# A convolution with an expert layer behind it: where the experts' weights are split into a high and a low part

## The chip, the cores and the metric

The kernel runs on one core of a Trainium2 chip. The core has five engines with a queue of instructions each: TensorE (PE, matrix products), VectorE (DVE), ScalarE (ACT), GpSimd (POOL) and SyncE (SP, which here only issues transfers). An engine takes its instructions strictly in the order in which they were put into its queue; a transfer is issued by an instruction in such a queue, too, and is then carried out by 16 DMA engines that all queues share. The metric is the device time of one execution in microseconds (us); less is better.

## The reference

A long convolution along the sequence, by Fourier transforms, and behind it a layer of eight experts of which each token takes one:

```python
Xf = np.fft.rfft(x, n=L, axis=1); Hf = np.fft.rfft(h, n=L, axis=0)
y = np.fft.irfft(Xf * Hf[None, :, :], n=L, axis=1)[:, :S, :]     # 8 x 5696 x 128
...
logits = y @ w_gate + modality_bias[modality_id]                 # 45568 tokens, 8 experts
e_idx = np.argmax(logits, axis=1)
...
for e in range(E):
    h = np.maximum(y[mask] @ w1[e], 0.0)                         # 128 -> 1024
    out[mask] = gate_w[mask, None] * (h @ w2[e])                 # 1024 -> 128
```

All is float32. The kernel makes a product of two float32 matrices out of three fast passes: each operand is split into a high part (the value rounded to the fast type, a ScalarE copy) and a low part (the value less its high part, a VectorE subtraction), and high x high, high x low and low x high are added up. For the experts this needs both parts of all weights.

## The kernel before

The batch is done in two groups of four sequences. **Stage 1** and **stage 2/3** (`stage1`, `stage23`) transform a group, multiply with the filter and transform back half way; `stage23` is a loop over 64 frequencies k, in which PE makes `px` (L261) and `pu` (L239), VectorE and GpSimd the products `t` (L264, L271), and ScalarE copies `pu` from the accumulators to `ut` (L244, and `hs`, L224), which is stored. **Stage 4** (`stage4`) finishes tokens, computes their expert and scatters each token as a row into a table sorted by expert. The **expert part** (`Moe`) then takes tiles of 512 tokens of one expert from that table. Its 104 tiles come in four levels, a level being what can be done with the tokens scattered so far: level 0 has 18 tiles, level 1 18, level 2 45, and level 3 23 small ones. Level 0 and 1 run beside the rest of stage 4; level 2 and 3 run alone.

An expert tile takes eight steps f (level 3: four). In a step PE makes three products into `ph` (`gemm1`, L567 to L569), ScalarE takes the high part of its positive values to `hh` (L572), VectorE the low part to `hl` (L573), and two steps later PE uses both in three products into `po` (`gemm2`, L589 to L591). `ph` has two buffers, so `gemm1` of step f+2 waits until `hl` of step f is done. The tile's weights lie in one of three slots (`slot`, 2 MB each with both parts of both matrices), used in turn; jobs are dealt so that a slot mostly keeps its expert, and the load of a slot (L543) is skipped when its expert stays the same.

`presplit` (L445 to L454) writes the split weights into a scratch in main memory, `w12s`, in 16 pieces: load 512 KB into `ws` (L450), ScalarE copy (L451), VectorE subtraction (L452), store 1 MB (L453). The transfers are issued from ScalarE's queue. There is one `ws` buffer, so a load waits until the store before has landed. `presplit` runs beside `stage23` of the second group (L673); the `0.25` there is its share in `run_all`, which deals out steps of several generators in turn.

What `run_all` fixes is the order in which work is written down. A scheduler then puts the instructions of PE, DVE, ACT and POOL into an order of its own, by its own estimate of times; in the expert part SP's queue alone keeps the order in which it was written.

Of the kernel before, what the change touches and what calls it, by code (L numbers as in the profile page):

```python
# [10 lines left out]
F32 = mybir.dt.float32  # L11
F32R = mybir.dt.float32r
# [3 lines left out]
ALU = mybir.AluOpType  # L16
AX = mybir.AxisListType
PACED = mybir.DependencyInfo(mybir.DependencyClass.Sync, mybir.DependencyReason.DATA)
PSUM = bass.MemoryType.PSUM
# [3 lines left out]
E, FF = 8, 1024  # L23
# [12 lines left out]
QA = 27  # L36
HP = 1000
PACE = 2
S4R = 5
RATE = 1.05  # L40
# [14 lines left out]
JOBS = [(lv, j) for lv, n in enumerate(LEVELS) for j in range(n)]  # L55
# [6 lines left out]
NSLOT = 3  # L62
# [19 lines left out]
def conv_moe(  # L82
# [5 lines left out]
    nc = tc.nc  # L88
# [353 lines left out]
            nc.vector.tensor_copy(bases[0], bases[1])  # L442


    def presplit(sp):  # L445
        for e in range(E):
            for a in range(2):
                s = sp.tile([128, 2, FF], F32R, name="ws")
                v = s.bitcast(F32)
                nc.scalar.dma_start(v[:, 1], w12_d[e, :, a])  # L450
                nc.scalar.copy(s[:, 0], v[:, 1])  # L451
                nc.vector.tensor_tensor(s[:, 1], v[:, 1], v[:, 0], op=ALU.subtract)  # L452
                nc.scalar.dma_start(w12s[e, :, a], v)  # L453
                yield  # L454


    padt = cp.tile([128, NSUB, RW], F32, name="padt")
# [62 lines left out]
    class Moe:  # L520
        def __init__(self, wp, sp, pst, psh, pso):
            self.sp, self.pst, self.psh, self.pso = sp, pst, psh, pso
            self.slots = [wp.tile([128, 2, 2, FF], F32R, name=f"slot{i}") for i in range(NSLOT)]
            self.st = {}
            self.outs = []
            self.tabs = {}

        def load(self, t):
# [6 lines left out]
            nc.sync.dma_start(rt[:, :ns], src[bass.ds(r0, ts), :].rearrange("(p c) w -> p c w", c=ns))  # L535
            self.st[t] = {"rt": rt, "ts": ts, "ns": ns}

        def load_weights(self, t):
            lv, j = JOBS[t]
            tab, n = self.tabs[lv][0], LEVELS[lv]  # L540
            ex = nc.sync.value_load(tab[0:1, n + j:n + j + 1], min_val=0, max_val=E - 1)
            ch = nc.sync.value_load(tab[0:1, 2 * n + j:2 * n + j + 1], min_val=0, max_val=1)
            nc.sync.dma_start(self.slots[t % NSLOT].bitcast(F32), w12s[bass.ds(ex, 1)].rearrange("o p a i f -> (o p) a i f"), cond=ch > 0)  # L543

# [74 lines left out]
        def run(self):  # L619
            LAG = 2  # L620
            total = len(JOBS)
            steps = []
            for t, (lv, j) in enumerate(JOBS):
                n = 4 if lv == len(LEVELS) - 1 else 8
                steps += [(t, f, n) for f in range(n)]
            self.load(0)
            self.load_weights(0)
            self.load(1)
            self.load_weights(1)
            self.load(2)  # L630
            self.prep(0)
            for g in range(len(steps) + LAG):
                t, f, n = steps[g] if g < len(steps) else (total, g - len(steps), 4)
                if f == 0 and t + 3 < total:
                    while JOBS[t + 3][0] not in self.tabs:
                        dispatch(4)
                        yield
                    self.load(t + 3)
                if t < total:
                    self.gemm1(t, f)  # L640
                    dispatch(1, self.st[t]["act"])
                    self.scatter(1, self.st[t]["act"])
                else:
                    self.scatter(1)
                if g >= LAG:
                    self.gemm2(*steps[g - LAG][:2])
                if f == LAG - 1 and t + 2 < total:
                    self.load_weights(t + 2)
                if t + 1 < total:
                    if f == (4 if n == 8 else 1):  # L650
                        self.prep(t + 1)
                if f == LAG and t >= 1:
                    self.finish(t - 1)
                yield
            if t < total or f < LAG:
                self.finish(total - 1)
            self.scatter(len(self.outs))
# [5 lines left out]
    with tc.tile_pool(name="p4", bufs=2, space=PSUM) as ps4, \  # L663
            tc.tile_pool(name="p4l", bufs=1, space=PSUM) as ps4l:
        with tc.tile_pool(name="s2", bufs=2) as sp2, tc.tile_pool(name="p2x", bufs=3, space=PSUM) as psx, \
                tc.tile_pool(name="p2u", bufs=2, space=PSUM) as psu:
            with tc.tile_pool(name="s1b", bufs=2) as sp1:
                run_all((stage23(0, sp2, psx, psu), 3), (stage1(1, sp1, ps4, ftab), 2))
            fx.close()
            tp = ctx.enter_context(tc.tile_pool(name="table", bufs=1, side="right"))  # L670
            sp4 = ctx.enter_context(tc.tile_pool(name="s4", bufs=2, side="right"))
            with tc.tile_pool(name="ws", bufs=1) as wsp:
                run_all((stage23(1, sp2, psx, psu), 3), (stage4(0, sp4, ps4, ps4l, 0, QA, True), S4R), (presplit(wsp), 0.25))  # L673
            dispatch(len(queue))

        def fence():

            nc.gpsimd.dma_start(rows_d[E * REGION:E * REGION + TS, :].rearrange("(p c) w -> p c w", c=NSUB), padt)

        ev = [None] * (len(LEVELS) + 1)  # L680
        with tc.tile_pool(name="moew", bufs=1) as wp, tc.tile_pool(name="moe", bufs=2) as sp, \
                tc.tile_pool(name="pm1", bufs=1, space=PSUM) as pst, tc.tile_pool(name="pm3", bufs=2, space=PSUM) as psh, \
                tc.tile_pool(name="pm2", bufs=2, space=PSUM) as pso, tc.manual_schedule(engines={mybir.EngineType.SP}):
            moe = Moe(wp, sp, pst, psh, pso)

            def level(lv, src):
                tab, ev[lv] = table(tp, lv, ev[lv - 1])
                moe.tabs[lv] = (tab, src)

            s4 = stage4(0, sp4, ps4, ps4l, QA, NQ)  # L690
            for _ in range(AHEAD):
                next(s4)
            fence()
            level(0, views[NVIEW])

            def rest():
                yield from s4
                while queue:
                    yield
                fence()  # L700
                level(1, views[NVIEW])
                yield from stage4(1, sp4, ps4, ps4l, 0, NQ)
                while queue:
                    yield
                padrow = tp.tile([1, E], I32, name="padrow")
                nc.vector.tensor_copy(padrow, bases[0][0:1, :])
                for e in range(E):
                    r0 = nc.sync.value_load(padrow[0:1, e:e + 1], min_val=e * REGION, max_val=e * REGION + NTOK)
                    nc.sync.dma_start(rows_d[bass.ds(r0, TS), :].rearrange("(p c) w -> p c w", c=NSUB), padt)
                level(2, rows_d)  # L710
                level(3, rows_d)
            run_all((rest(), RATE), (moe.run(), 1))


def _constants():
# [80 lines left out]
```

## Time and profile before

| what | us |
|---|---|
| median of 3 runs | 2305.79 (2302.34 to 2326.87) |
| profiled execution | 2318.76, its span 2317.0 |
| stage 2/3 of the second group, with `presplit` in it | 391 to 665 |
| the same stage after `presplit` has ended | 665 to 865 |
| level 0 of the experts beside stage 4 | 890 to 1245 |
| level 1 beside stage 4 | 1245 to 1520 |
| level 2, alone (a stretch of it) | 1560 to 2060 |

The stretches are read from the first and last instructions of the lines named above. In the profile an engine is busy while an instruction of its own computes; issuing a transfer, or standing at an instruction that waits, does not count as busy. TensorE runs at one of two clocks, and the granted clock of a stretch is the mean, with 1.00 for full speed. Matmuls overlap in the profile, so a busy time of PE is read as an upper bound, and its waits are the better measure of what it loses.

### The profile page before, as it was taken

How to read it: one execution, taken by the hardware profiler on the slowest of the kernel's cores; microseconds unless marked ns; L12 is line 12 of the kernel's file. 1: busy time of each engine (PE TensorE's matmuls, PEld its weight loads, DVE VectorE, ACT ScalarE, POOL GpSimd, SP SyncE). 2: the span in 40 equal slices, each digit the busy share in tenths (PEclk: the TensorE clock that was granted, in tenths of full speed). 3: DMA queues.
4: the chain of work that ended last, by engine and by line, in shares of the span. 5: the costliest groups of instructions: out<-in, count | busy, mean ns of one | idle time of the engine just before them, and what ended most of it. 6: DMA issues, size and time to landing. Idle time of an engine off the chain costs nothing.

```text
span 2317.0 us, 33168 instructions
## 1 busy us (share of the span) xinstructions
PE 2107.8 (91%) x9598; PEld 1502.3 (65%) x9598; DVE 1466.0 (63%) x2473; ACT 1132.8 (49%) x2010; POOL 1085.6 (47%) x1050
## 2 busy tenths in 40 slices
PE   6779999899999897999899989889999999999997
PEld 5655555334444445777677667667888888888886
DVE  6559999776777984576465555555555555555443
ACT  6557776333333343555455555334444444444433
POOL 2126655344777763665665556553333333333222
PEclk9899999999999997999999999979999999999999
DMA  9999989899997765433244432132111121123331
GB/s 338 325 307 318 312 293 301 290 314 320 300 282 240 230 193 214 130 109 113 88 149 149 150 101 85 55 123 80 44 47 42 45 82 44 45 80 109 106 104 56
DMA packets 198309, 388.89 MB, mean 168 GB/s; under 512 B 32757, under 2 KB 63833, under 8 KB 193776
## 3 DMA queue, kind: packets, MB, share of 16 engines
q1 hardware_dynamic: 148832, 276.81, 36.5%
q10 hardware_dynamic: 25776, 62.34, 8.5%
q0 software_dynamic: 23520, 47.61, 6.2%
q8 instruction: 78, 1.28, 0.2%
q14 instruction: 103, 0.84, 0.1%
HBM read 393.95 MB, written 174.21 MB: 245 GB/s over the span
## 4 chain that ended last, share of the span: by engine, by line
PE 56%; issue 3%; ACT 2%; DVE 2%; another core or an unknown queue 2%; DMA 1%; POOL 1%; SPq 0%; POOLq 0%; ACTq 0%; DVEq 0%
PE ph L567 8%; PE ph L569 7%; PE po L589 7%; PE po L590 7%; PE po L591 7%; PE ph L568 7%; PE py L357 4%; PE pxt L602 2%; PE pxt L550 2%; PE py L364 1%; PE pl L371 1%; DVE hl L573 1%; ACT hh L572 1%; PE pu L239 1%
## 5 line engine op out<-in xcount | busy, mean ns | idle before, releaser
L573 DVE SCALAR_TENSOR_TENSOR hl<-ph,hh 128x512 fp32r<-128x512 f32 x740 | 506.7, 689 | 457.1 <-ACT hh L572 361.7
L572 ACT ACTIVATE hh<-ph 128x512 fp32r<-128x512 f32 x740 | 440.9, 599 | 600.0 <-PE ph L569 410.5
L613 POOL DMA_INDIRECT out<-of,mrt x370 | 363.1, 981 | 576.7 <-ACT hh L572 475.5
L298 POOL DMA_INDIRECT rows<-rt,idx x360 | 375.3, 1042 | 274.5 <-ACT hh L572 163.5
L271 POOL TENSOR_TENSOR t<-t,t 96x512 f32<-96x512 f32 x212 | 296.7, 1416 | 223.9 <-DVE t L264 214.4
L589 PE MATMUL po<-hh,slot 128*128 128x512 f32 (+1 forms) x832 | 328.3, 395 | 42.3 <-ACT hh L572 25.7
L264 DVE TENSOR_TENSOR t<-px,hs 96x512 f32<-96x512 f32 x512 | 318.2, 676 | 61.5 <-PE pu L239 17.4
L567 PE MATMUL ph<-mxh,slot 128*128 128x512 f32 (+1 forms) x832 | 331.1, 398 | 17.7 <-DVE hl L573 8.1
L590 PE MATMUL po<-hl,slot 128*128 128x512 f32 (+1 forms) x832 | 313.4, 377 | 0.1
L569 PE MATMUL ph<-mxh,slot 128*128 128x512 f32 (+1 forms) x832 | 312.1, 375 | 0.8 <-issue 0.8
L568 PE MATMUL ph<-mxl,slot 128*128 128x512 f32 (+1 forms) x832 | 312.7, 376 | 0.0
L591 PE MATMUL po<-hh,slot 128*128 128x512 f32 (+1 forms) x832 | 310.6, 373 | 0.0
L261 PE MATMUL px<-z,m 96*96 96x512 f32 x512 | 261.5, 610 | 11.1 <-DVE t L264 5.8
L589 PEld LDWEIGHTS po<-hh,slot 128*128 128x128 f32 x832 | 159.3, 192 | 82.4 <-ACT hh L572 36.5
L244 ACT COPY ut<-pu 90x512 f32<-90x512 f32 x256 | 145.0, 583 | 132.6 <-PE pu L239 60.3
L239 PE MATMUL pu<-t,mi 96*96 96x512 f32 x352 | 182.9, 625 | 20.7 <-ACT ut L244 11.4
L567 PEld LDWEIGHTS ph<-mxh,slot 128*128 128x128 f32 x832 | 159.7, 192 | 53.9 <-DVE hl L573 18.5
L590 PEld LDWEIGHTS po<-hl,slot 128*128 128x128 f32 x832 | 158.8, 191 | 35.5 <-DVE hl L573 2.7
L569 PEld LDWEIGHTS ph<-mxh,slot 128*128 128x128 f32 x832 | 159.1, 191 | 31.4 <-issue 0.5
L591 PEld LDWEIGHTS po<-hh,slot 128*128 128x128 f32 x832 | 158.7, 191 | 30.0
L568 PEld LDWEIGHTS ph<-mxl,slot 128*128 128x128 f32 x832 | 159.9, 192 | 23.6 <-issue 0.5
L261 PEld LDWEIGHTS px<-z,m 96*96 96x96 f32 x512 | 82.2, 166 | 115.4 <-issue 64.3
(157 smaller groups left out, 2892.2 us busy)
## 6 DMA issues: line engine op xcount, KB each, us to landing
slot<-w12s SPq DMA_DIRECT2D x104, 2048.0 KB
z<-z SPq DMA_DIRECT2D x256, 180.0 KB
z<-z SPq DMA_DIRECT2D x90, 320.0 KB
z<-z SPq DMA_DIRECT2D x90, 256.0 KB
ua<-ut SPq DMA_DIRECT2D x128, 180.0 KB
ub<-ut SPq DMA_DIRECT2D x128, 180.0 KB
mrt<-rows SPq DMA_DIRECT2D x81, 260.0 KB
w12s<-ws ACTq DMA_DIRECT2D x16, 1024.0 KB
```

The lines of the kernel that those rows point to most:

```text
L261: nc.tensor.matmul(px[:KP], mm, zbuf[i][k % NZ], start=True, stop=True)
L264: nc.vector.tensor_tensor(prod[i, j].rearrange("p (b d) -> p b d", d=D), px[:KP].rearrange("p (b d) -> p b d", d=D), hs[:, j, k % KH].unsq ...
L298: d = nc.gpsimd.indirect_dma_start(views[count[0] % NVIEW], bass.IndirectOffsetOnAxis(ap=idx[:, t:t + 1], axis=0), rt[:, t, :], None, boun ...
L567: nc.tensor.matmul(po, w[:, 0, 0, fs], st["xh"], start=True, stop=False)
L568: nc.tensor.matmul(po, w[:, 0, 0, fs], st["xl"], start=False, stop=False)
L569: nc.tensor.matmul(po, w[:, 0, 1, fs], st["xh"], start=False, stop=True)
L572: st["act"] = nc.scalar.activation(hh, ph, AF.Relu)
L573: nc.vector.scalar_tensor_tensor(hl, ph, 0.0, hh.bitcast(F32), op0=ALU.max, op1=ALU.subtract)
L589: nc.tensor.matmul(po, w[:, 1, 0, fs], hh[:, cs], start=k == 0, stop=False)
L590: nc.tensor.matmul(po, w[:, 1, 0, fs], hl[:, cs], start=False, stop=False)
L591: nc.tensor.matmul(po, w[:, 1, 1, fs], hh[:, cs], start=False, stop=k == 7)
L613: d = nc.gpsimd.indirect_dma_start(oviews[(t * NSUB + c) % NVIEW], bass.IndirectOffsetOnAxis(ap=ri[:, c, D + 1:D + 2], axis=0), of[:, c, : ...
```

## The change

Two things are done. The splitting of all weights moves: `presplit` no longer runs in stage 2/3 of the second group but beside the expert part, behind `rest()` and `moe.run()` at a share of 0.6, so that its 64 steps lie within the 144 steps of level 0. Its pieces are half as large (32, with 256 KB in and 512 KB out), its transfers go into SP's queue, and load and split are written down one step apart. And the tiles of level 0 cannot use the scratch, since it is not there yet: each loads its expert's plain weights, 1 MB, without the condition that skipped a load, into one buffer `raw`, and splits them into its slot by two ScalarE copies and two VectorE subtractions (`split_weights`), for tile t+2 in step 5 of tile t.

```diff
     def presplit(sp):
         for e in range(E):
             for a in range(2):
-                s = sp.tile([128, 2, FF], F32R, name="ws")
-                v = s.bitcast(F32)
-                nc.scalar.dma_start(v[:, 1], w12_d[e, :, a])
-                nc.scalar.copy(s[:, 0], v[:, 1])
-                nc.vector.tensor_tensor(s[:, 1], v[:, 1], v[:, 0], op=ALU.subtract)
-                nc.scalar.dma_start(w12s[e, :, a], v)
-                yield
+                for c in range(2):
+                    cs = slice(c * FF // 2, (c + 1) * FF // 2)
+                    s = sp.tile([128, 2, FF // 2], F32R, name="ws")
+                    v = s.bitcast(F32)
+                    nc.sync.dma_start(v[:, 1], w12_d[e, :, a, cs])
+                    yield
+                    nc.scalar.copy(s[:, 0], v[:, 1])
+                    nc.vector.tensor_tensor(s[:, 1], v[:, 1], v[:, 0], op=ALU.subtract)
+                    nc.sync.dma_start(w12s[e, :, a, :, cs], v)
+                    yield
...
+        def split_weights(self, t):
+            if JOBS[t][0] == 0:
+                s = self.slots[t % NSLOT]
+                v = self.raw.pop(t)
+                for a in range(2):
+                    nc.scalar.copy(s[:, a, 0], v[:, a])
+                    nc.vector.tensor_tensor(s[:, a, 1], v[:, a], s.bitcast(F32)[:, a, 0], op=ALU.subtract)
+
         def load_weights(self, t):
...
+            if lv == 0:
+                v = self.raw[t] = self.wp.tile([128, 2, FF], F32, name="raw")
+                nc.sync.dma_start(v, w12_d[bass.ds(ex, 1)].rearrange("o p a f -> (o p) a f"))
+                return
...
                 if f == LAG - 1 and t + 2 < total:
                     self.load_weights(t + 2)
+                if f == 5 and t + 2 < total:
+                    self.split_weights(t + 2)
...
-            with tc.tile_pool(name="ws", bufs=1) as wsp:
-                run_all((stage23(1, sp2, psx, psu), 3), (stage4(0, sp4, ps4, ps4l, 0, QA, True), S4R), (presplit(wsp), 0.25))
+                run_all((stage23(1, sp2, psx, psu), 3), (stage4(0, sp4, ps4, ps4l, 0, QA, True), S4R))
...
-            run_all((rest(), RATE), (moe.run(), 1))
+            run_all((rest(), RATE), (moe.run(), 1), (presplit(wsp), 0.6))
```

What the scheduler makes of it is seen in the order of the built programs. ScalarE's queue in stage 2/3 of the second group, in the kernel before (`ut` and `hs` are the copies that free PE's accumulators):

```order
L450 DMA ws<-in_w 128x1024
L224 COPY hs<-pu 96x256
L244 COPY ut_3824<-pu 90x512
L244 COPY ut_3829<-pu 90x512
L451 CAST ws<-ws 128x1024
L244 COPY ut_3848<-pu 90x512
L244 COPY ut_3853<-pu 90x512
L453 DMA w12s<-ws 128x2048
```

In the changed kernel the three lines of `presplit` are gone from this place, and the copies follow each other:

```order
L244 COPY ut_3848<-pu 90x512
L244 COPY ut_3853<-pu 90x512
L224 COPY hs<-pu 96x256 x2
L244 COPY ut_3882<-pu 90x512
L244 COPY ut_3887<-pu 90x512
```

ScalarE's queue within level 0 of the changed kernel, where `hh` is the copy of each expert step and `uh`, `rt` and `ys` belong to stage 4:

```order
L592 ACTIVATE hh<-ph 128x512 x2
L550 CAST slot_7333<-raw 128x1024 x2
L375 CAST ys_9440<-py 128x512
L341 DMA u<-ua 128x512
L342 DMA u<-ub 128x512
L360 COPY rt<-py 128x4x128
L346 CAST uh<-u 128x1024
L323 CAST gt<-gs 128x3x128
L592 ACTIVATE hh<-ph 128x512
L456 CAST ws<-ws 128x512
L592 ACTIVATE hh<-ph 128x512
```

The rows of L550 and L456 are new there; before, the same kinds of rows stood next to each other without them. SP's queue at the same level, before (`mrt` are a tile's tokens):

```order
L535 DMA mrt<-rows 128x520
L541 TENSOR_LOAD tab_7529
L541 ISA x2
L542 TENSOR_LOAD tab_7529
L542 ISA x2
L543 ISA
L543 DMA slot_7415<-w12s 128x4096
```

And in the changed kernel, from one tile's tokens to the next:

```order
L542 DMA mrt<-rows 128x520
L556 TENSOR_LOAD tab_7448
L556 ISA x2
L559 ISA
L559 DMA raw<-in_w 128x2048
L454 DMA ws<-in_w 128x512
L458 DMA w12s<-ws 128x2x512
L454 DMA ws<-in_w 128x512
L458 DMA w12s<-ws 128x2x512
L454 DMA ws<-in_w 128x512
```

Between the loads of tokens and weights there now stand loads of pieces, each of which waits for the store before it, and stores, each of which waits for its subtraction.

## Rows read from the trace of the kernel before

**Rows 1.** The page's shares of the chain of work that ended last, by engine.

```profile
PE 56%; issue 3%; ACT 2%; DVE 2%; another core or an unknown queue 2%; DMA 1%; POOL 1%; SPq 0%; POOLq 0%; ACTq 0%; DVEq 0%
```

**Rows 2.** Four stretches of the span: length, busy time of PE, of its weight loads, of DVE, ACT and POOL (with numbers of instructions), granted clock, share of the DMA engines, GB/s.

```profile
391.00:665.00 274.00, 251.40 (x712) 108.98 (x713) 198.09 (x315) 102.70 (x195) 146.60 (x131) 0.94 0.93 307
665.00:775.00 110.00, 105.79 (x346) 48.97 (x344) 87.01 (x168) 41.78 (x80) 81.76 (x72) 0.98 0.82 251
890.00:1245.00 355.00, 323.48 (x1662) 254.05 (x1660) 202.62 (x432) 184.53 (x332) 209.37 (x214) 0.96 0.40 129
1560.00:2060.00 500.00, 499.27 (x2307) 404.00 (x2306) 280.99 (x412) 240.46 (x412) 160.08 (x166) 1.00 0.18 53
```

**Rows 3.** What PE waited for from 391 to 665: line and tile that waited, what it waited for, us in total, times, longest. It has nine rows, which come to 22.3 us; the first three and the last:

```profile
PE pu L239 <- ACT ut L244: 8.6, 7, 2.4
PE pu L239 <- ACT ex L415: 3.7, 1, 3.7
PE pu L239 <- ACT hs L224: 3.0, 2, 2.5
...
PE px L261 <- DVE t L264: 0.4, 1, 0.4
```

**Rows 4.** The same from 665 to 775, when `presplit` has ended.

```profile
PE py L364 <- ACT rt L360: 1.4, 1, 1.4
PE pu L239 <- ACT ut L244: 1.3, 1, 1.3
PE px L261 <- issue: 0.9, 1, 0.9
PE px L261 <- PE px L261: 0.5, 1, 0.5
```

**Rows 5.** What ACT waited for from 391 to 665, the rows that name a transfer's landing just ahead of a copy.

```profile
ACT ws L451 <- DMA ws<-in_w: 31.5, 13, 4.7
ACT ut L244 <- DMA ua<-ut: 12.2, 5, 4.9
...
ACT hs L224 <- DMA ub<-ut: 5.4, 2, 4.6
...
ACT tot L413 <- DMA w12s<-ws: 4.4, 1, 4.4
...
ACT ut L244 <- DMA w12s<-ws: 3.6, 1, 3.6
...
ACT ex L415 <- DMA w12s<-ws: 2.7, 1, 2.7
```

**Rows 6.** The instructions of `presplit`, by its tile: duration in ns (least, median, most), first and last start.

```profile
L450 ACTq DMA_DIRECT2D ws<-in_w x16: 346/352/385, 391.3 to 651.7; - x16
L451 ACT CAST ws<-ws x16: 1029/1045/1047, 398.1 to 658.0; 128x1024 fp32r<-128x1024 f32 x16
L452 DVE TENSOR_TENSOR ws<-ws x16: 1210/1225/1860, 399.2 to 659.0; 128x1024 fp32r<-128x1024 f32 x16
L453 ACTq DMA_DIRECT2D w12s<-ws x16: 338/339/381, 402.4 to 660.3; - x16
```

**Rows 7.** Pieces of the order of time, first in ACT's queue and PE's around 410, then around 613: start, duration, instruction, and in brackets its engine's idle time before it and what ended it.

```profile
410.40 0.35 ACTq L450 DMA_DIRECT2D ws<-in_w  x1
410.79 0.37 ACT L224 COPY hs<-pu 96x256 f32<-96x256 f32 x1 [4.60 <-DMA ub<-ut]
411.21 1.17 PE L239 MATMUL pu<-t,mi 96*96 96x512 f32 x1 [2.47 <-ACT hs L224]
...
609.71 2.95 DVE L400 TENSOR_TENSOR lg<-lg,mx 128x96 f32<-128x96 f32 x1
613.50 1.17 PE L239 MATMUL pu<-t,mi 96*96 96x512 f32 x1 [3.68 <-ACT ex L415]
```

**Rows 8.** Level 0 (890 to 1245) by line, ACT and DVE: times, busy us and mean ns of one, idle time before and what ended it.

```profile
L572 ACT ACTIVATE hh<-ph 128x512 fp32r<-128x512 f32 x146 | 86.4, 601 | 116.9 <-PE ph L569 59.8 <-remote 12.7 <-PE po L591 12.6
L346 ACT CAST uh<-u 128x1024 fp32r<-128x1024 f32 x30 | 31.6, 1052 | 4.1 <-PE py L357 2.9 <-PE ph L569 1.2
L347 DVE TENSOR_TENSOR ul<-u,uh 128x1024 fp32r<-128x1024 f32 x30 | 36.7, 1225 | 45.1 <-ACT uh L346 36.8 <-issue 3.5 <-PE ph L569 2.3
L555 DVE TENSOR_TENSOR mxl<-pxt,mxh 128x512 fp32r<-128x512 f32 x18 | 12.4, 687 | 5.8 <-ACT mxh L554 2.4 <-issue 2.2 <-ACT yt L367 0.9
```

**Rows 9.** What PE waited for in level 0.

```profile
PE po L589 <- ACT hh L572: 11.1, 6, 2.9
...
PE ph L567 <- DVE hl L573: 2.5, 7, 1.0
```

**Rows 10.** The start of level 0 in order of time: SP's issues and PE's first uses.

```profile
876.80 0.39 SPq L535 DMA_DIRECT2D mrt<-rows  x1
878.97 0.38 SPq L543 DMA_DIRECT2D slot<-w12s  x1
879.82 1.08 PE L550 MATMUL pxt<-ident,mrt 128*128 128x128 f32 x4 [3.11 <-DMA mrt<-rows]
886.85 0.77 PE L567 MATMUL ph<-mxh,slot 128*128 128x512 f32 x1 [5.95 <-DMA slot<-w12s]
```

**Rows 11.** Sizes of transfers by issue, from the page's table and the longer one: KB each.

```profile
slot<-w12s SPq DMA_DIRECT2D x104, 2048.0 KB
mrt<-rows SPq DMA_DIRECT2D x81, 260.0 KB
```

More of the change, by code (lines that the diff above doesn't have):

```diff
@@ L442, in stage4 @@
             nc.vector.tensor_copy(bases[0], bases[1])
+    split_done = []
     def presplit(sp):
@@ L447, in presplit @@
             for a in range(2):
-                s = sp.tile([128, 2, FF], F32R, name="ws")
-                v = s.bitcast(F32)
-                nc.scalar.dma_start(v[:, 1], w12_d[e, :, a])
-                nc.scalar.copy(s[:, 0], v[:, 1])
-                nc.vector.tensor_tensor(s[:, 1], v[:, 1], v[:, 0], op=ALU.subtract)
-                nc.scalar.dma_start(w12s[e, :, a], v)
-                yield
+                for c in range(2):
[8 more added lines that the diff above has]
+                    yield
+        split_done.append(True)
     padt = cp.tile([128, NSUB, RW], F32, name="padt")
@@ L525, in __init__ @@
             self.outs = []
+            self.wp, self.raw = wp, {}
             self.tabs = {}
@@ L541, in load_weights @@
             ex = nc.sync.value_load(tab[0:1, n + j:n + j + 1], min_val=0, max_val=E - 1)
+            if lv == 0:
+                v = self.raw[t] = self.wp.tile([128, 2, FF], F32, name="raw")
+                nc.sync.dma_start(v, w12_d[bass.ds(ex, 1)].rearrange("o p a f -> (o p) a f"))
+                return
+            assert split_done
             ch = nc.sync.value_load(tab[0:1, 2 * n + j:2 * n + j + 1], min_val=0, max_val=1)
@@ L627, in run @@
             self.load_weights(0)
+            self.split_weights(0)
             self.load(1)
@@ L631, in run @@
             self.prep(0)
+            self.split_weights(1)
             for g in range(len(steps) + LAG):
@@ L682, in conv_moe @@
                 tc.tile_pool(name="pm1", bufs=1, space=PSUM) as pst, tc.tile_pool(name="pm3", bufs=2, space=PSUM) as psh, \
-                tc.tile_pool(name="pm2", bufs=2, space=PSUM) as pso, tc.manual_schedule(engines={mybir.EngineType.SP}):
+                tc.tile_pool(name="pm2", bufs=2, space=PSUM) as pso, \
+                tc.tile_pool(name="ws", bufs=1) as wsp, tc.manual_schedule(engines={mybir.EngineType.SP}):
             moe = Moe(wp, sp, pst, psh, pso)
```

## The prediction

> **What bounds the kernel now.** I read the chain of work that ended last first, to see which engine sets the end: PE has 56% of the span on it and no other engine over 2% [rows 1]. So the time is PE's own work, which the change leaves as it is, and what PE loses between its instructions. The next view is therefore the table of stretches, and in it the granted clock and the other engines' busy time [rows 2]. From 1560 to 2060, with the experts alone, PE is busy for 499 of 500 us at clock 1.00: nothing is lost there. From 391 to 665, where the splitting runs, the clock is 0.94, and from 890 to 1245, level 0, it is 0.96. The third view is what PE waited for. In 391 to 665 the waits come to 22.3 us, nearly all on ScalarE's copies [rows 3]; in 665 to 775, the same loop with the splitting ended, to 4.1 us [rows 4]. The last is what ScalarE itself waited for [rows 5]: 31.5 us on the loads of `ws`, and the order of time shows a second kind: at 410.40 ScalarE could issue the next load only once the store before had landed, so the copy behind it came 4.60 us late, and PE stood 2.47 us for that copy [rows 7]. A transfer in ScalarE's queue that has to wait holds all copies behind it.
>
> **What the removal gives.** Waits of PE: at the rate of the stretch without splitting, 4.1 us in 110, 274 us would have 10.2, so 22.3 - 10.2 = 12.1 go. Clock: 0.94 against 0.98 over 274 us is 16.4 - 5.5 = 10.9 us [rows 2]. Together 23.0 us. The lower bound is 12, with the clock as it was: 3.68 us of the waits have another cause, a VectorE instruction of 2.95 us at 609.71 for which ScalarE stood [rows 7], but the rate without splitting contains such things too. The upper bound is 33, all waits and the clock's part. The DMA engines, 93% busy there, lose 25 MB of traffic and stand nowhere on PE's list, so nothing is put down for them. Nor for the edges: what takes the place of the pieces in ScalarE's queue is the next copies.
>
> **What level 0 gets.** ScalarE gets 36 copies of 128x1024 (18 tiles, two each) at 1.052 us, as L346, and 32 of 128x512 at 0.60, as L572: 37.9 + 19.2 = 57 us. VectorE gets 36 subtractions at 1.225, as L347, and 32 at 0.687, as L555: 44.1 + 22.0 = 66 us [rows 8]. Their busy time goes from 184.5 to 242 and from 202.6 to 269 of 355 us [rows 2]. That leaves idle time on both, so busy time alone doesn't lengthen the level; what does is that a copy of `hh` or an `hl` comes later while PE needs it. PE already stands for `hh` six times (11.1 us) and for `hl` seven times (2.5 us) there [rows 9], so there is little slack, and the step is short: 146 steps in 355 us [rows 8] are 2.43 us each, while two raw copies in a row take 2.10 and their subtractions 2.45.
>
> To this come waits of ScalarE for the loads, since it meets each cast in a fixed order: 18 for `raw` and 32 for `ws`. In 391 to 665 a wait was 31.5 / 16 = 2.0 us, the DMA engines 93% busy; in level 0 they are 40% busy at 129 GB/s [rows 2], and the moved 25 MB and the raw 19 MB add 124 GB/s over 355 us, so by the same ratio nearly 80%. I take half, 1.0 us each: 50 us. ScalarE is then taken for 57 + 50 = 107 us.
>
> What PE loses per us of this is read from the old place. There ScalarE was taken for 16 casts (16.7 us), 32 issues (11.1 us) [rows 6], 31.5 us of loads and 28.3 us of the other five rows [rows 5], 87.6 us in all, and PE lost 23.0: 0.26 per us. Counting only casts and load waits, 48.2 us, it is 0.48. So level 0 loses 28 to 51 us. I take 42, nearer the upper end: in the old place VectorE's subtraction stood on nobody's way, here it stands ahead of `hl`. The lower bound is none (all of it fits between the steps), the upper is the third rival's 65.
>
> The other edits come to nothing. **Start of the level:** the first slot, 2048 KB, was there 7.88 us after its issue, `mrt` with 260 KB after 3.02 [rows 10, 11]; so 1 MB takes about 3.02 + 764/1788 x 4.86 = 5.1 us, and a copy of 1.05 and a subtraction of 1.23 follow before the third product: within 1 us of before. Nothing hides it, and it is there once. **SP's queue:** behind a waiting store stand the next tile's tokens and weights. Tokens are loaded three tiles ahead, some 58 us, so nobody waits for those; weights two tiles ahead and split four steps (10 us) after their load is written down, which the 1.0 us above stands for. **Skipped loads:** level 0 loads 18 MB in any case where some 2 MB loads were skipped; that is in the ratio above. **Level 1** finds the scratch ready: the last piece is written down in tile 13 of 18, and what the scheduler puts off is done by step 120 of 144.
>
> **Sum.** 2318.8 - 23.0 + 42 = 2337.8 for the profiled execution. That one lies 13.0 over the median of the runs (2305.8), so the median goes to 2324.8, or 2325.
>
> **Rivals.** *Faster: level 0 takes the splits in its idle time.* For it: from 1560 to 2060 ScalarE is 48% and VectorE 56% busy and PE loses nothing [rows 2], and both keep over 85 us idle in level 0. Against it: the waits that PE has there already [rows 9]. It needs loads that land before their cast is reached, so that the 50 us of waits fall to under 10. Level 0 then loses under 5 us, and the time is 2305.8 - 23 + 3 = 2286, or down to 2275 with the upper bound of the gain.
>
> *Slower: SP's queue paces level 0.* A piece is a chain: load, copy, subtraction, store, and only then the next load, since there is one buffer. By the rows the load takes 3.0 us (260 KB), copy and subtraction 1.3, the store of 512 KB 3.02 + 252/1788 x 4.86 = 3.7, issues 0.3: 8.3 us [rows 8, 10, 11]. Each tile's `raw` and `mrt`, 1284 KB at 368 KB per us, put 3.5 us into the same queue. 32 x 8.3 + 13.4 x 3.5 = 313 us, where the order of ScalarE's queue in the built program puts the pieces' casts at steps 9 to 120, 111 x 2.43 = 270 us. The 43 us over are waits of ScalarE that no slack takes up, and with 57 us of copies at 0.26 and some 7 us of clock level 0 loses 65: 2305.8 - 23 + 65 = 2348. It decides from about 9 us a piece on.
>
> *Slower: VectorE and GpSimd get in each other's way.* One subtraction of L452, beside GpSimd's products, took 1.860 us where the median is 1.225 [rows 6]. In level 0 GpSimd works 209 of 355 us, but the like subtraction L347 has a mean of 1.225 [rows 8], so nothing shows it there. If all 36 were so long, VectorE would have 23 us more ahead of `hl`, and about half of that would reach PE: 2337. The Trainium skill, GPSIMD Engine Reference, section Specifications, says that GpSimd shares its ways into SBUF with VectorE and that they contend where VectorE has two inputs from SBUF, as these subtractions do; by that rule the splits would run slower at the new place, while the mean of L347 beside GpSimd's scatters says that they don't.
>
> **How the numbers follow.** About 1% (23 us) is what a measurement of this kernel can tell from no change; the three runs of before lie that far apart. Forecast, 2325, with level 0 losing 20 to 46 us: 0.42, nearly all within 1%. Faster: 0.20. SP's queue: 0.28. VectorE and GpSimd: 0.10. Faster by over 1% (under 2283) is most of the first rival, 0.19; slower by over 1% (over 2329) is the second and third and the forecast's upper edge, 0.41; within 1% is 0.40. The range runs from 2278, a gain of 28 with level 0 unharmed, to 2368, level 0 losing 85 where stores under load take 1 us longer than the rows say and the clock falls to 0.93. The forecast alone has 2303 to 2335.
>
> **What would show it.** The stage of the second group ends some 20 us earlier, PE's list of waits there loses the rows on `ut` and `hs` above 2 us, and the clock from 391 on is 0.97 or more; if it stays at 0.94, the gain is 12. In level 0 (it begins some 20 us earlier), ScalarE's waits on `raw` and `ws` come to about 50 us in 50 waits: under 10 speaks for the first rival, over 90 for the second, and there SP's own waits are for landings of `w12s` throughout. PE's waits on `hh` and `hl` in level 0 rise by 25 us or more and the level takes about 395 us. L551, the subtraction on `raw`, takes 1.23 us unless the third rival holds. The rest, from level 1 on, keeps its length; if that moves by more than 5 us, the scheduler's other order is a cause that I have left out.

## The result and the profile after

| | before | changed |
|---|---|---|
| median of 4 runs | 2311.36 (2302.34 to 2326.87) | 2344.90 (2337.62 to 2350.42) |
| ratio, 95% interval | | 1.012 (1.0084 to 1.0155) |
| profiled execution, its span | 2318.76, 2317.0 | 2346.89, 2345.0 |
| first product of level 0 | 886.8 | 849.1 |
| first product of level 1 | 1237.3 | 1264.7 |
| first product of level 2 | 1587.2 | 1615.2 |
| level 0, level 1, the rest | 350.5, 349.9, 729.8 | 415.6, 350.5, 729.8 |

The changed kernel is slower by 33.5 us in the medians, by some 28 by the ratio and by 28.1 in the profiled executions. (The table's median of before is that of four runs; the forecast started from 2305.8, that of three.) The starts of the levels (the first `ph` product of tiles 0, 18 and 36) account for all of the last: level 0 begins 37.7 us earlier, takes 65.1 us longer, level 1 takes 0.6 longer and the rest nothing. 65.1 + 0.6 - 37.7 = 28.0.

The chain of work that ended last, by engine, first:

```profile
PE 45%; DMA 5%; issue 5%; DVE 4%; ACT 4%; another core or an unknown queue 2%; POOL 2%; SPq 0%; ACTq 0%; POOLq 0%; DVEq 0%
```

PE has lost 11 points of it, and the transfers, VectorE and ScalarE have gained [rows 1]: somewhere PE now stands for what is behind them. The stretches of the changed kernel, columns as in [rows 2]: the old place and level 0.

```profile
391.00:640.00 249.00, 244.88 (x747) 110.31 (x746) 191.17 (x310) 94.53 (x186) 152.15 (x138) 1.00 0.82 251
849.00:1265.00 416.00, 348.44 (x1639) 264.94 (x1638) 256.24 (x492) 231.23 (x394) 208.81 (x207) 0.89 0.60 195
```

The same row for level 0 of the kernel before, cut at its own two ends:

```profile
887.00:1237.00 350.00, 319.74 (x1637) 251.26 (x1638) 199.24 (x423) 182.22 (x326) 203.27 (x207) 0.96 0.41 132
```

At the old place PE's clock is 1.00 where it was 0.94. In level 0 PE has the same instructions (1639 and 1637), but is busy for 28.7 us more, since the clock fell from 0.96 to 0.89, and idle for 67.6 us where it was idle for 30.3: 37.3 more. So of the 66 us between these two rows a little under half is not waiting at all, but the same products at a lower clock, in a level that now has more gaps.

What PE waited for at the old place, 391 to 640 (these are all rows):

```profile
PE px L261 <- DVE t L264: 1.9, 2, 1.0
PE pl L411 <- DVE oh L406: 0.8, 1, 0.8
PE py L352 <- DMA u<-ua: 0.5, 1, 0.5
PE px L261 <- issue: 0.5, 1, 0.5
```

The waits on `ut`, `hs` and `ex` of [rows 3] are gone: 3.7 us are left of 22.3. What it waited for in level 0, 851 to 1250:

```profile
PE po L609 <- ACT hh L592: 21.1, 16, 3.2
PE pxt L570 <- DVE of L625: 6.7, 5, 2.3
PE pxt L622 <- issue: 6.3, 2, 3.8
PE ph L587 <- DVE hl L593: 6.2, 14, 1.1
...
PE ph L587 <- ACT slot L550: 2.8, 2, 1.7
...
PE ph L589 <- DVE slot L551: 1.8, 1, 1.8
```

The waits of [rows 9] have grown, for `hh` from 11.1 us in 6 to 21.1 in 16, for `hl` from 2.5 in 7 to 6.2 in 14. For the split weights themselves (`slot`) PE stands only 4.6 us: the tiles are ready in time, and what comes late is the everyday work behind the splits. ScalarE's list for the same stretch shows why:

```profile
ACT ws L456 <- DMA ws<-in_w: 30.1, 14, 5.2
ACT hh L592 <- remote: 23.0, 6, 4.2
ACT slot L550 <- DMA raw<-in_w: 14.8, 7, 3.7
```

One of those waits in order of time, as in [rows 7]:

```profile
1012.58 0.62 ACT L456 CAST ws<-ws 128x512 fp32r<-128x512 f32 x1 [2.60 <-DMA ws<-in_w]
...
1013.10 0.59 ACT L592 ACTIVATE hh<-ph 128x512 fp32r<-128x512 f32 x1
...
1013.59 0.15 ACT L413 CAST tot<-pl 96x1 bf16<-96x1 f32 x1
...
1013.74 0.49 PE L609 MATMUL po<-hh,slot 128*128 128x512 f32 x1 [1.79 <-ACT tot L413]
```

ScalarE stands 2.60 us at the cast of a piece for its load. `hh` and `tot` are behind it, and PE, which wants them, stands 1.79 us. The cast itself is 0.62. At 410 the old place had a like picture [rows 7], with an issue at the head in place of a cast; it has moved, not gone.

SP's waits from 840 to 1250, the three largest rows:

```profile
SPq L458 <- DVE ws L457: 143.8, 21, 13.3
SPq L454 <- DMA w12s<-ws: 35.5, 13, 5.8
SPq L542 <- DMA out<-of,mrt: 13.0, 2, 10.5
```

SP stands mostly at the store of a piece (L458), for its subtraction, up to 13.3 us; meanwhile the loads written behind that store cannot be issued. Last, the splits by tile: ns of one, least, median and most.

```profile
L456 ACT CAST ws<-ws x32: 602/619/633, 867.5 to 1199.7; 128x512 fp32r<-128x512 f32 x32
L457 DVE TENSOR_TENSOR ws<-ws x32: 668/685/693, 869.1 to 1201.2; 128x512 fp32r<-128x512 f32 x32
...
L550 ACT CAST slot<-raw x36: 1036/1045/1098, 847.6 to 1220.9; 128x1024 fp32r<-128x1024 f32 x36
L551 DVE TENSOR_TENSOR slot<-raw,slot x36: 1206/1218/1227, 848.6 to 1222.9; 128x1024 fp32r<-128x1024 f32 x36
```

None is longer than its like elsewhere [rows 6, 8].

### The profile page after: what moved, and what is told of

The parts are those of the page before. It is cut to its first block, busy times and chain, and to the rows that moved or that the text cites. A ratio compares the mean times of both kernels' runs of the same rounds, so it can differ in the third digit from the quotient of the medians.

```text
span 2345.0 us, 33252 instructions
## 1 busy us (share of the span) xinstructions
PE 2115.2 (90%) x9598; PEld 1510.1 (64%) x9598; DVE 1504.4 (64%) x2525; ACT 1171.6 (50%) x2062; POOL 1085.8 (46%) x1050
## 4 chain that ended last, share of the span: by engine, by line
PE 45%; DMA 5%; issue 5%; DVE 4%; ACT 4%; another core or an unknown queue 2%; POOL 2%; SPq 0%; ACTq 0%; POOLq 0%; DVEq 0%
PE ph L587 7%; PE ph L589 6%; PE po L609 6%; PE po L610 6%; PE po L611 6%; PE ph L588 6%; PE py L357 2%; PE pxt L622 2%; DMA raw<-in_w 2%; PE pxt L570 1%; DMA ws<-in_w 1%; DVE hl L593 1%; ACT hh L592 1%; POOL rows L298 1%
## 5 line engine op out<-in xcount | busy, mean ns | idle before, releaser
L264 DVE TENSOR_TENSOR t<-px,hs 96x512 f32<-96x512 f32 x512 | 319.4, 676 | 74.5 <-PE pu L239 37.3
L261 PE MATMUL px<-z,m 96*96 96x512 f32 x512 | 259.2, 605 | 13.4 <-DVE t L264 6.9
L239 PE MATMUL pu<-t,mi 96*96 96x512 f32 x352 | 173.6, 598 | 2.0 <-ACT ut L244 1.8
L261 PEld LDWEIGHTS px<-z,m 96*96 96x96 f32 x512 | 81.5, 165 | 111.7 <-issue 64.8
```

The source lines that it names most:

```text
L261: nc.tensor.matmul(px[:KP], mm, zbuf[i][k % NZ], start=True, stop=True)
L264: nc.vector.tensor_tensor(prod[i, j].rearrange("p (b d) -> p b d", d=D), px[:KP].rearrange("p (b d) -> p b d", d=D), hs[:, j, k % KH].unsq ...
```

## Experiments

The theory to test is that of the prediction, **waiting**: the splits cost time because ScalarE meets casts whose loads are late. Its rivals: **work** (the added copies and subtractions themselves come ahead of `hh` and `hl`), **buffer** (one `ws` buffer makes each piece a chain that SP's queue paces), and, for the old place, **queue** (what cost time there was that the transfers were issued from ScalarE's queue).

The runs went to four chips. The kernel before takes 2218 us on one of them and 2306 to 2321 on the others, so each difference below is to the kernel before on the same chip, and comparisons across chips are marked as such. "Start" and "length" are of level 0 in the profiled execution.

| run | chip's before | this | difference | start | length |
|---|---|---|---|---|---|
| e1_two_buffers | 2218.04 | 2259.68 | +41.6 | 842.3 | 392.1 |
| e2_raw_alone | 2218.04 | 2292.71 | +74.7 | 888.4 | 381.4 |
| e3_pieces_alone | 2218.04 | 2282.24 | +64.2 | 885.5 | 368.0 |
| e4_old_place_sp_queue | 2218.04 | 2222.11 | +4.1 | 896.3 | 304.9 |
| b_again | 2305.53 | 2307.97 | +2.4 | 882.1 | 352.0 |
| a_again | 2305.53 | 2336.35 | +30.8 | 843.6 | 409.9 |
| e5_raw_first | 2305.53 | 2315.91 | +10.4 | 885.4 | 364.4 |
| e6_both_early | 2305.53 | 2314.31 | +8.8 | 844.7 | 394.9 |
| e7_raw_alone_again | 2320.56 | 2359.29 | +38.7 | 883.0 | 393.5 |
| e8_pieces_alone_again | 2320.56 | 2377.07 | +56.5 | 883.5 | 413.3 |
| e9_tokens_later | 2320.56 | 2310.14 | -10.4 | 847.8 | 385.6 |
| e10_pieces_no_transfers | 2312.31 | 2315.22 | +2.9 | 886.0 | 353.1 |

e2, e3, e5, e7, e8, e10 and b_again are single executions; the others have 4 or 10 runs. Runs of one kernel on one chip lie up to 17 us apart (2298.6 to 2315.4 for the kernel before where e5 ran), so a difference of some 8 us in a single execution says little. The expectations of e1 to e3 were written for a level 0 of 350.5 us. Where they ran, a level 0 without splits takes 304.9 (e4), so they are read here by what is added to that.

### One part at a time

**e1_two_buffers**: the changed kernel with two `ws` buffers, each load written one piece ahead of its cast.

```diff
-                    nc.sync.dma_start(v[:, 1], w12_d[e, :, a, cs])
+            if n + 1 < len(todo):
+                held = load(*todo[n + 1])
+            yield
...
-                ot = self.sp.tile([128, TS], F32, name="ot")
+                ot = self.sp.tile([128, TS], F32, name="ot", bufs=1)
...
-                tc.tile_pool(name="ws", bufs=1) as wsp, tc.manual_schedule(engines={mybir.EngineType.SP}):
+                tc.tile_pool(name="ws", bufs=2) as wsp, tc.manual_schedule(engines={mybir.EngineType.SP}):
```

> The changed kernel with two ws buffers and the load of a piece written down ahead of the split of the piece before (to make room, one buffer for ot instead of two). Level 0, from the first ph product of tile 0 to that of tile 18, took 350.5 us before and 415.6 after. If ScalarE's standing for late loads costs this (waiting theory), its waits on ws fall from 30 us to under 10 and level 0 to 385 us or less. If the copies and subtractions themselves do, ahead of hh and hl (work theory), level 0 stays at 405 us or more.

It is 1.0202 (1.0171 to 1.0232) of the kernel before on its chip, and ScalarE still waits, 844 to 1230:

```profile
ACT ws L462 <- DMA ws<-in_w: 37.6, 20, 3.7
ACT slot L556 <- DMA raw<-in_w: 29.6, 14, 3.9
```

The loads come as late as with one buffer (the change, on its chip), where the waiting theory had said under 10 us, and level 0 is 87.2 us longer than in e4, which by the rule on record speaks for work. But what was to make the loads early did not do so, and waiting is not tested by it. The single buffer alone is not what makes the loads late.

**e2_raw_alone**: the split of the level-0 tiles on arrival, with `presplit` as before the change at its old place.

```diff
-            run_all((rest(), RATE), (moe.run(), 1), (presplit(wsp), 0.6))
+            run_all((rest(), RATE), (moe.run(), 1))
...
+            with tc.tile_pool(name="ws", bufs=1) as wsp:
+                run_all((stage23(1, sp2, psx, psu), 3), (stage4(0, sp4, ps4, ps4l, 0, QA, True), S4R), (presplit(wsp), 0.25))
```

> The splitting of all weights is put back to where it was before (stage 2/3 of the second group, ScalarE's queue, 16 whole pieces); only the splits of raw weights stay in level 0. Level 0 should start at about 885 us, as before. Work theory: raw has 38 of the 57 us of copies and 44 of the 66 us of subtractions, two thirds of the 65 us lost, so level 0 takes 393 us. Waiting theory: raw had 18 of ScalarE's 48 us of load waits, so 375 us.

ScalarE's waits on `raw` here, and SP's largest row (875 to 1265):

```profile
ACT slot L546 <- DMA raw<-in_w: 53.0, 15, 6.7
```

```profile
SPq L538 <- DMA out<-of,mrt: 299.0, 28, 20.0
```

With nothing but the level-0 tiles to split, ScalarE waits longer for `raw` than in the whole change. L538 is the load of tokens, three tiles ahead. It needs a buffer that an earlier tile holds until its results have landed, and SP stands there up to 20 us. The load of weights for the tile after next stands behind it in the same queue, though its deadline is the nearer one. Level 0 is 76.5 us longer than in e4, more than either theory had put on it (work 42.5, waiting 24.5).

**e3_pieces_alone**: the kernel before, which also splits the 32 pieces a second time beside level 0, into a scratch `w12x` that nobody reads.

```diff
-            run_all((rest(), RATE), (moe.run(), 1))
+            run_all((rest(), RATE), (moe.run(), 1), (pieces(wsp), 0.6))
```

> The kernel before, with the 32 pieces done a second time beside level 0 as in the change, into a second scratch that nobody reads; no raw splits. Work theory: pieces have a third of the copies, so level 0 takes 372 us. Waiting theory: they had 30 of the 48 us of load waits, and SP's chain paces the level, so 390 us or more.

Level 0 is 63.1 us longer than in e4, where work had been put at 21.5 and waiting at 39.5 or more. The pieces alone cost 64.2 us on this chip, and raw alone 74.7. The two parts are not additive: both together cost 41.6 net in e1, where level 0 starts 43 to 46 us earlier than in e2 and e3, and that is a gross loss of 85 to 88.

**e4_old_place_sp_queue**: the kernel before, with the transfers of `presplit` issued from SP.

```diff
-                nc.scalar.dma_start(v[:, 1], w12_d[e, :, a])
+                nc.sync.dma_start(v[:, 1], w12_d[e, :, a])
...
-                nc.scalar.dma_start(w12s[e, :, a], v)
+                nc.sync.dma_start(w12s[e, :, a], v)
```

> The kernel before, with the transfers of presplit issued from SP's queue in place of ScalarE's; all else as before. Level 0 began at 886.8 us before and at 849.1 with the pieces gone. If what cost PE there was ScalarE standing at transfers in its own queue (queue theory), level 0 begins by 862 us and the kernel takes some 25 us less than before, about 2286. If it was the traffic and the copies themselves, level 0 begins at 875 us or later and the time is within 12 us of before. SP's queue also carries the loads of z and the stores of ut; if a store of w12s that waits for its subtraction holds those, level 0 begins later than 887.

1.0014 (1.0001 to 1.0026): nothing is won, and level 0 starts 8 to 11 us later than in e2 and e3, which split at the old place from ScalarE's queue (its profile is of the slowest of its ten runs). From 391 to 665 the clock is again 0.94, and ScalarE has this row:

```profile
ACT ws L451 <- DMA ws<-in_w: 38.0, 13, 5.1
```

The issues have left ScalarE's queue, but the cast has not, and it still stands for its load, 38.0 us against 31.5 [rows 5]; all of PE's waits there come to 19.9 us against 22.3 [rows 3]. The queue theory falls as the main cost. SP's queue carries the stores of `ut` too, and what the transfers hold up there in place of ScalarE's copies was not separated.

### The place of the loads in SP's queue

**b_again, a_again**: the two kernels once more, as a base on a second chip.

> The kernel before, unchanged, with a profile from the chip of these experiments, where it takes 2218 us in place of 2306. Level 1 was 52 to 60 us shorter in the four experiments than in the first profiles, with no waits of ScalarE put down to another core or an unknown queue. Both theories expect the same here: level 0 starts at 880 to 890 us and takes about 305 us, and level 1 about 295.

> The changed kernel, unchanged, on the same chip. If the waits put down to an unknown queue had hidden part of the cost on the first chip, level 0 loses more than the 65 us there, 80 to 95, the level starts 37 to 45 us earlier, and the ratio is 1.02; if they have nothing to do with it, the ratio is 1.012 as there.

Their starts differ by 38.5 us and their level 0 by 57.9, not by the 80 to 95 of a hidden cost; the change costs 1.0138 (1.0108 to 1.0168). The 305 us of level 0 that I expected of the kernel before is that of the fast chip; here it is 352.0.

**e5_raw_first**: e2 with the load of the weights written ahead of the load of tokens.

```diff
+                if f == 0 and t + 2 < total and JOBS[t + 2][0] == 0:
+                    self.load_weights(t + 2)
...
-                if f == LAG - 1 and t + 2 < total:
+                if f == LAG - 1 and t + 2 < total and JOBS[t + 2][0]:
```

> As e2 (raw splits alone in level 0), but the load of raw for tile t+2 is written down in step 0 ahead of the load of the tokens of tile t+3, and not behind it in step 1. In e2 SP stood 314 us within level 0 at the loads of tokens, whose buffer is freed by the scatter of an older tile, and ScalarE 53 us at the raw loads behind them. Waiting theory: ScalarE's waits on raw fall under 10 us and level 0 from 381 to about 325 us. Work theory: level 0 stays at 365 us or more, since all copies and subtractions are still there.

**e7_raw_alone_again**: e2 unchanged, on another chip.

> e2 again (raw splits alone, raw's load behind that of the tokens), since e2 and e5 ran on two chips on which level 0 of the kernel before differs by nearly 50 us. On a chip like that of e5, where the kernel before takes 2306 us and level 0 352 us: waiting theory, level 0 takes 390 us or more here against 364 in e5, with 40 us or more of ScalarE's waits on raw; work theory, within 10 us of e5.

ScalarE's waits on `raw` in level 0, in e5 and then in e7:

```profile
ACT slot L546 <- DMA raw<-in_w: 3.5, 2, 2.8
```

```profile
ACT slot L546 <- DMA raw<-in_w: 35.3, 12, 7.1
```

SP's largest row in e7, at the loads of tokens:

```profile
SPq L538 <- DMA out<-of,mrt: 180.7, 17, 19.2
```

The copies, subtractions and bytes are the same in both kernels; the load of `raw` has moved one step forward, ahead of that of the tokens. ScalarE's waits fall from 35.3 (53.0 in e2) to 3.5 us, and the cost from 38.7 (74.7) to 10.4. What is left, 12.4 us in level 0 against b_again on the same chip, bounds the work of 36 copies and subtractions, as far as single executions tell. By the numbers on record e7 is where waiting had it (390 us or more, though the waits are under its 40 us), and e5 at the 365 us of work; but the numbers for e5 were written for the chip of e2. How much of the difference is the chip's can't be told from e5 against e7, which ran on two; that e2 and e7, one kernel, differ by 36 us in cost says that it can be a lot. The next run has its base on the same chip.

**e6_both_early**: e1 with the same move.

> e1 (two ws buffers, loads a piece ahead) with the raw loads ahead of the tokens as in e5. Waiting theory: level 0 falls from 392 to about 350 us and the kernel is within 1% of before; work theory: level 0 stays at 385 us or more and the kernel 2% slower.

2314.31 against 2336.35 for the change on the same chip: 22.0 us come back, with all the work and all the bytes in place. e6 also has the second `ws` buffer of e1, so what the order alone gives is not told. It stands at 1.0037 (1.0018 to 1.0057) of the kernel before. ScalarE's rows of this kind in a_again (842 to 1260) and then in e6, and SP's in e6:

```profile
ACT ws L456 <- DMA ws<-in_w: 25.9, 15, 5.1
ACT slot L550 <- DMA raw<-in_w: 20.9, 11, 3.5
```

```profile
ACT ws L462 <- DMA ws<-in_w: 62.5, 23, 8.3
...
ACT slot L556 <- DMA raw<-in_w: 15.7, 9, 3.5
```

```profile
SPq L548 <- DMA out<-of,mrt: 118.6, 16, 13.3
SPq L451 <- DMA w12s<-ws: 71.1, 17, 7.9
```

`raw` is waited for somewhat less; the loads of the pieces now take their turn behind the waiting load of tokens. The result is a mixed one: the time is within 1%, as waiting had it, and level 0 takes 394.9 us, as work had it. And ScalarE's load waits have grown from 46.8 to 78.2 us in sum while level 0 is 15.0 us shorter, so this sum alone does not measure the loss.

**e9_tokens_later**: e6, with the load of tokens in level 0 moved from step 0 to step 6, where its buffer is nearly free.

```diff
-                if f == 0 and t + 3 < total:
+                if f == (6 if JOBS[t % total][0] == 0 else 0) and t + 3 < total:
```

> e6 (two ws buffers, raw's load first) with the tokens of tile t+3 loaded in step 6 of tile t and not in step 0, for level 0, when their buffer is free. In e6 SP stood 118 us at these loads and ScalarE 62 us at ws loads behind them. Waiting theory: ScalarE's waits on ws fall under 20 us, level 0 from 395 to about 370 us, and the kernel is 0.5% faster than before; work theory: level 0 stays at 390 us.

0.9965 (0.994 to 0.999) of the kernel before: the only version that is faster than it, by 10.4 us. SP's wait on that load is down to 44.6 us in 7, and ScalarE's on the pieces to 42.8 in 21. Its level 0 has a clock of 0.92 and still takes 385.6 us. Waiting had said under 20 us of waits on the pieces and 370 us, work 390; the waits and the length came less than half way. e6 and e9 ran on two chips, so what the move of the tokens alone gives is not told.

### Work or waiting, for the pieces

**e8_pieces_alone_again**: e3 unchanged.

> e3 again (pieces alone), for the same reason. On a chip where level 0 of the kernel before takes 352 us, work theory: 352 + 20 = 372 us; waiting theory: 390 us or more, as SP's chain of load, split, store and next load gives the pace; ScalarE waits 25 us or more on ws.

**e10_pieces_no_transfers**: the kernel before with the 32 copies and subtractions of e8 on a tile that is there from the start. It loads and stores no piece. To spread the copies, each is bound behind the `hh` written down last (`add_manual_dep`); in e8 nothing binds them. They start from 901 to 1145, in e8 from 897 to 1236.

```diff
-                    nc.sync.dma_start(v[:, 1], w12_d[e, :, a, cs])
-                    yield
-                    nc.scalar.copy(s[:, 0], v[:, 1])
+            c = nc.scalar.copy(s[:, 0], v)
+            if acts:
+                tc.add_manual_dep(c.ins, acts[-1].ins.name, PACED, reason="spacing")
...
-                    nc.sync.dma_start(w12x[e, :, a, :, cs], v)
```

> The kernel before, with the 32 copies and 32 subtractions of the pieces beside level 0, spread over steps 9 to 107 as the change spreads them, but on a tile that is loaded once: no load and no store per piece, and nobody reads the results. With its transfers, this set made level 0 413 us in e8. Work theory: the copies and subtractions cost most of that, so level 0 takes 395 us or more on a chip where it takes 352 before (350 or more where it takes 305). Waiting theory: they fit between the steps, and level 0 is within 10 us of before.

Level 0 of e8 and then of e10, columns as in [rows 2]:

```profile
884.00:1296.00 412.00, 339.00 (x1627) 260.19 (x1626) 220.03 (x450) 200.06 (x357) 200.83 (x208) 0.90 0.52 171
```

```profile
886.00:1239.00 353.00, 325.55 (x1638) 256.05 (x1639) 216.20 (x453) 199.92 (x357) 207.88 (x208) 0.94 0.39 131
```

VectorE and ScalarE have the same number of instructions, within three, and busy times within 4 us. With the transfers the level takes 413.3 us, without them 353.1, where the kernel before takes 350.5 or 352.0 (all on slower chips, but not on the same one). On the fast chip, e3 and e4 differ by 63.1 us. So the work of the pieces costs 1 to 3 us, and about 60 come with their transfers: the work theory falls. Both runs are as waiting had them, e8 with 30.1 us of ScalarE's waits on `ws`. But not all of the 60 us in e8 hangs on these loads. PE's largest row there is for `ot`, ScalarE's copy of a tile's result, and the trace does not name what ScalarE stood for ahead of it:

```profile
PE pxt L617 <- ACT ot L609: 19.3, 6, 8.1
```

```profile
ACT ot L609 <- remote: 18.5, 3, 9.3
```

e3 has no such row among its largest.

## Why the prediction went as it did

The sign was right, and the mechanism too as far as the runs go: ScalarE stands for loads of the splits, and `hh` behind it comes late. 2344.9 lies in the range, 20 us above the forecast, of which 5.6 are the higher median of before. But it is outside the forecast's own case (to 2335; by its 20 to 46 us of loss that case ends at 2329), slower by over 1% where this case had put nearly all within 1%, and next to the 2348 of the second rival. That the profiled execution is only 9.1 us above its forecast (2346.9 against 2337.8) is in part luck: two terms were mis-sized, by 14.7 and 23.1 us, and their errors partly cancel.

**The gain at the old place, 23.0 forecast, 37.7 measured.** The step that failed is the clean rate. I read what the loop loses without splitting from 665 to 775 [rows 4], and took off 10.2 us of waits and 5.5 of clock for it. The changed kernel shows the stretch of the splits itself without them: 3.7 us of waits, clock 1.00. And the part of the loop that I had taken as the measure loses as much as before, though no split ever ran ahead of it: counted in order, the products `px` (L261) are 2.5 us later than before at 406, 34.6 us earlier at 670 and 34.7 at 780, so all is gained where the pieces ran. From 640 to 750 the changed kernel has a clock of 0.97 and 6.0 us of waits (all rows):

```profile
PE px L261 <- DVE t L264: 1.9, 1, 1.9
PE pu L239 <- ACT ut L244: 1.5, 1, 1.5
PE py L364 <- ACT rt L360: 1.2, 1, 1.2
PE px L261 <- issue: 0.9, 1, 0.9
PE px L261 <- PE px L261: 0.5, 1, 0.5
```

It is a part with losses of its own. Without that subtraction the rows give 22.3 - 3.7 = 18.6 of waits and 0.06 x 274 = 16.4 of clock, 35 us. The last `pl` product ahead of level 0 is at 840.95 in place of 876.42, 35.5 us earlier, so that is the gain; the other 2.3 us are at the start of the level. The bound of 33 that I called the upper one was too low, since it held only part of the clock.

**ScalarE's time for the splits, 57 us of copies and 50 of load waits, forecast.** Measured: 35.0 us for 35 of the 36 raw copies, 19.8 for the 32 pieces, and 44.9 us of waits (30.1 and 14.8), in 21 waits where I had thought of 50 short ones. Right.

**What PE loses for it, 42 forecast, 65.1 measured.** The step that failed is the loss per us, 0.26 to 0.48. It had the gain in its numerator. With 37.7 in the place of 23.0 it is 37.7 / 87.6 = 0.43, or 0.78 by the narrower count, so 46 to 84 us, which holds what came. That it lies in the middle proves neither count, and e4 speaks against the wider one: with the issues out of ScalarE's queue PE waits nearly as much. The one wrong rate went into both terms; the loss, on the larger base, took the larger error. And a rate for all of ScalarE's taken time hides what the runs separate: the copies and subtractions themselves cost little (for the pieces 1 to 3 us, for `raw` some 12.4 at most), and the rest comes with their transfers.

**The clock.** I counted it where it would come back; in level 0 it stands in the forecast only inside the rate per us, of whose 23.0 us it was 10.9. There it fell from 0.96 to 0.89, 28.7 us more for the same instructions, a little under half of the loss.

**The rivals.** *Level 0 takes the splits in its idle time*: not in this kernel, but its condition, loads that land before their cast, is nearly what e5 gives `raw`, and there the cost is 10.4 us. *SP's queue paces level 0* had the right price, 65, but not for its reason. A piece came every 10.7 us (867.5 to 1199.7), over the 9 from which it was to decide, but SP waits 143.8 us for subtractions and 35.5 for landings, ScalarE's load waits are 45 and not over 90, and a second buffer, which breaks the chain, left them (e1, on another chip). But SP's queue is where loads get late. I had passed over it with "Tokens are loaded three tiles ahead, some 58 us, so nobody waits for those". In e2 and e7 nobody waits for the tokens, but the weights behind them do. In the change itself SP stands only 13.0 us at tokens; there it is the stores of the pieces, at which it stands 143.8, that hold the loads behind them. *VectorE and GpSimd*: L551 has a median of 1.218 us and a most of 1.227, L457 0.685 and 0.693, as their likes [rows 8]. By the rule of the Trainium skill, GPSIMD Engine Reference, section Specifications, they contend with GpSimd; beside level 0's scatters none became longer.

**The small terms.** The start of the level was costed at nothing and gained 2.3 us: from the last `pl` product to the first into `ph` it takes 8.14 us (840.95 to 849.09), before 10.43 (876.42 to 886.85, 5.95 of it PE's wait for the slot [rows 10]). The first product stands for no slot any more. The 1 MB of `raw` landed at 847.57, 5.05 us after its issue (forecast 5.1), and the first copy was done by 848.64, while PE stood 3.19 us, until 848.36, for the tokens of the second tile. Level 1 and the rest kept their length, to 0.6 and 0.0 us, so the scheduler's other order costs nothing there. Of the other signs on record, the start of level 0, the clock and the rows at the old place came; PE's waits on `hh` and `hl` rose by 13.7 us and not by 25 or more, and the level takes 415.6 and not 395.

**Open.** For the pieces, e10 takes away both the late loads and 25 MB of traffic, so the two are not separated, and it fixes the place of the copies besides. That e6 is 22.0 us faster than a_again with the same traffic shows that order and buffers of the transfers matter, but not through which wait, since ScalarE's load waits grew. Taking the traffic away with the waits kept was not tried. Why e2 costs 74.7 us on one chip and 38.7 on another is not settled either.

## What to carry to other kernels

Work that is moved off a busy stage cost little here where its operands were there when the in-order engine reached it, and held up what is queued behind it where they were not: look at the deadline of each load, and put a load with a near deadline ahead of one that has to wait for a buffer in the same queue. Read the price of such a disturbance against the same part of the loop without it (by an order of the work that shows it, or as none at all and as a neighbour's, for a range), not against a neighbouring part that has losses of its own, since one rate then sizes both the gain and the loss. Where PE stands for many short waits, count the clock as a term beside them.

## What was not expected of the hardware

The kernel before takes 2218 us on one chip and 2306 to 2321 on three others. Between e4 on the first (whose level 0 does the same work as before's) and b_again on the second, level 0 is 304.9 and 352.0 us and level 1 298.0 and 341.6, while the stretch behind level 1 takes 729.9 and 730.5. The slower one has waits of ScalarE in level 0 that the trace puts down to another core or an unknown queue; in b_again, 884 to 1230:

```profile
ACT hh L572 <- remote: 18.4, 4, 5.9
ACT yt L367 <- remote: 16.8, 4, 5.8
```

In the first nothing of this kind stands among the largest rows. What they wait for no run shows.

The other is the share of the clock: gaps of at most 3.8 us, 67.6 us of them in 416, came with a granted clock of 0.89, and 30.3 in 350 with 0.96. The 0.92 of e9 lies between, with 385.0 - 336.1 = 48.9 us idle. The idle time does not fix it: e10 has 27.5 in 353 with 0.94.
